# Linear attention and a GLU feed-forward layer on one core: x in a ring with two transfer queues, and some weight sums, loads and stores moved

## The chip, the cores and the metric

The kernel runs on one core of a Trainium2 chip. A core has TensorE (PE, matrix products, with its weight loads listed as PEld), VectorE (DVE), ScalarE (ACT), GpSimd (POOL) and SyncE (SP), each with its own queue of instructions that it takes in order, and 16 DMA engines. DMAs are issued by ACT, POOL or SP. The metric is the time of one execution on the device in microseconds (us); the median of several executions is compared.

## What is computed

q, k and v are float32 of shape (8, 8, 576, 64): batch, head, sequence, head dimension. All weights are float32 as well.

```python
kv = np.einsum('bhsd,bhse->bhde', k, v)
out = np.einsum('bhsd,bhde->bhse', q, kv)
rms = np.sqrt(np.mean(out * out, axis=-1, keepdims=True) + 1e-06)
out = out / rms * g_norm
x = out.transpose(0, 2, 1, 3).reshape(8 * 576, 512)      # 4608 tokens
gate = 1.0 / (1.0 + np.exp(-(x @ w_gate)))               # 512 x 1536
val = x @ w_val                                          # 512 x 1536
y = (gate * val) @ w_out                                 # 1536 x 512
```

## The kernel before

**Chunks and batches.** The feed-forward part runs over 9 chunks (c = 0 to 8) of 512 tokens. A batch of the attention gives 576 tokens, so batches and chunks don't end together. Batches 0 and 1 come at the start; the attention of batch c + 1 is woven into chunk c, for c = 1 to 6. Chunks 7 and 8 have no attention beside them.

**Products.** Chunk 0 is computed with plain matrix products. Chunks 2 to 8 use a fast scheme of the Strassen kind in both layers: the blocks of the matrices are added and subtracted first, and 26 products of these sums take the place of 32. In the first layer (`first_layer_fast`, L926) there are three blocks j of 26 products each, numbered p = 26 j + i; in the second layer (`second_layer_fast`, L1032) there are 26 products with the index i, done in the order 0, 3, 1, 2, 6, 4, 5, 7, 8 and so on up. Chunk 1 has the fast first layer and a plain second one (`second_layer_plain`, L1005). After a product, `combine` adds its PSUM tile to outputs and to temporaries: copies on ACT (L893), sums on DVE (L897) and gate products on POOL (L889, with the sigmoid on ACT, L886). A PSUM tile that later products go on with is first copied or added away; the copy after product 4 of the second layer and the product 7 that goes on in the same tile are such a pair.

**Sums of the inputs.** The sums of x for a chunk (18 operations on DVE, L825 and L827) are made in the second layer of the chunk before. They are put at step p0 of this layer, two a step up to the sum number `two`, then one a step. The sums of the first-layer weights (28 for each block j, `w1_sums`, L739, on POOL) are made once. Those for block 2 are all queued before chunk 1 begins. The weights and their sums are then stored to DRAM in chunk 1 (`keep_w1`, L753, by POOL), and from chunk 2 on they are read back in four granules per block (`load_granule`, L765, by POOL), of 768 or 896 KB. A granule is loaded when the products of the one before it in its place are done. The second-layer weights come the same way (`load_w`, L971).

**Attention.** `feed(c + 1)` gives the steps of a batch, and lists of places hang each on a product. The k and v of a batch come by `load_late`, called at the end of the chunk before: eight main loads (L118), then four smaller ones for the rest of the sequence (L123), all on SP. The q of a pair of heads comes by `load_q` (L104), also on SP, issued when the turn of the pair before is done; so it stands behind these loads in SP's queue. For two pairs of heads at a time, `two_pairs` computes the outputs and their norm, and `x_turn` brings them into the layout that the products want: two transposes on DVE (L432) into `xTs`, then DMAs within SBUF into the tile of x of a chunk (L442, SP). These break at the ends of chunks, so that one `x_turn` has four to six of them. The first two pairs of heads have their `x_turn`s in the first layer, the other two theirs in the second layer, after the 5th and 6th step (`at2` 4 and 5; in chunk 1, 4 and 8).

**Stores.** Each row block of y is stored by SP (L495, L502); only the last one's left half in chunk 8 is shared by SP and ACT.

Of the kernel before, what the change touches and what calls it, by code (L numbers as in the profile page):

```python
# [10 lines left out]
FP32 = mybir.dt.float32  # L11
# [9 lines left out]
def kernel(  # L21
# [11 lines left out]
    nc = tc.nc  # L33
# [75 lines left out]
    def load_late(b):  # L109


        if b >= B:
            return
        mains = {}
        for n in range(NHP):
            for name, src in (("k", k), ("v", v)):
                mains[n, name] = t = kv_place(len(mains))
                nc.sync.dma_start(out=t.rearrange("p (h c) -> p h c", h=2),  # L118
                                  in_=src[b, 2 * n:2 * n + 2, 0:S4].rearrange("h (p j) d -> p h (j d)", j=NK4))
        rest = kv_place(len(mains))  # L120
        for i, src in enumerate((k, v)):
            for r in range(2):
                nc.sync.dma_start(out=rest[PH * r:PH * r + PH, GH * i:GH * i + GH].rearrange("p (h d) -> p h d", d=HD),  # L123
                                  in_=src[b, NHP * r:NHP * r + NHP, S4:S].rearrange("h p d -> p h d"))
        kv_late[b] = mains, rest

# [128 lines left out]
    nc.scalar.activation(out=sb.tile([P, 1], FP32, name="unused", bufs=1), in_=eps, func=AF.Sqrt)  # L255


    xT = {}

    def chunk(c):  # L260
        if c not in xT:
            xT[c] = sb.tile([P, NMT, G], FP32, tag="xT", name="xT", bufs=3)
        return xT[c]

    def attention(n, at_ps):
# [88 lines left out]
    def feed(b):  # L354
# [30 lines left out]
            if e == 1:  # L385
                load_q(n + 1)

        def two_pairs(n0):


            d = {}
            ms = sb.tile([P, NQ, NJ], FP32, tag="ms2", name="ms2", bufs=1)
            sq = sqs[:, 0:2 * S].rearrange("p (r c) -> p r c", r=NQ)
            units = [slice(NJ // 2 * i, NJ // 2 * (i + 1)) for i in range(2)]

            def by_head(t):
                return t.rearrange("p r (n d) -> p r n d", d=HD)

            def u_mm():
                d["u"] = u = at_ps()[:, 0:NQ, 0:2 * QC]  # L400
                for which in range(2):
                    for g in range(JH):
                        for i in range(NC):
                            for r in range(NQ):
                                for e in range(2):
                                    c, o = NJ * HD * e + QC * i + PH * g, HD * (JH * which + g)
                                    nc.tensor.matmul(u[HD * e:HD * e + HD, r, o:o + HD],  # L407
                                                     qTs[QB * r:QB * r + QB, (n0 + which) % 2, c:c + PH],
                                                     kvq[QB * r:QB * r + QB, (n0 + which) % NHP, NC * e + i],
                                                     start=(i == 0), stop=(i == NC - 1))  # L410

            def u_square():
                nc.scalar.activation(out=sq, in_=d["u"], func=AF.Square)

            def u_sum(i):
                nc.vector.tensor_reduce(out=ms[:, :, units[i]], in_=by_head(sq)[:, :, units[i]], axis=AX.X, op=ALU.add)

            def u_root():
                nc.scalar.activation(out=ms, in_=ms, func=AF.Sqrt, bias=eps, scale=1.0 / HD)

            def u_norm(i):
                if i == 0:
                    nc.vector.reciprocal(ms, ms)
                m_ = ms[:, :, units[i]]
                nc.vector.tensor_tensor(out=by_head(sq)[:, :, units[i]], in0=by_head(d["u"])[:, :, units[i]],
                                        in1=m_.unsqueeze(3).to_broadcast([P, NQ, NJ // 2, HD]), op=ALU.mult)

            def x_turn(i):


                for which in range(2):
                    nc.vector.transpose(xTs[:, i, which],  # L432
                                        sq.rearrange("p r (w g i c) -> p w i r g c", w=2, g=JH, i=NC)[:, which, i])
                m = n0 % NHP
                for j in range(2):
                    for e in range(2):
                        p0, p1 = HD * e + QB * j, HD * e + QB * i
                        s0 = 0
                        while s0 < S // 2:
                            c, o = divmod(S * b + S // 2 * j + s0, G)  # L440
                            n_ = min(G - o, S // 2 - s0)
                            nc.sync.dma_start(out=chunk(c)[p1:p1 + QB, m:m + 2, o:o + n_],  # L442
                                              in_=xTs[p0:p0 + QB, i, :, s0:s0 + n_])
                            s0 += n_

            return ([u_mm, u_square, lambda: u_sum(0), lambda: u_sum(1), u_root, lambda: u_norm(0), lambda: u_norm(1)] +
                    [lambda i=i: x_turn(i) for i in range(NC)])
# [4 lines left out]
        n0 = NHP * b  # L452
        kv = [kv_mm] + [lambda i=i: kv_copies(i, range(3)) for i in range(2 * NC)]
        t0, t1, t2, t3 = (turns_of(n0 + i) for i in range(4))
        u0, u1 = two_pairs(n0), two_pairs(n0 + 2)
        first = list(zip((1, 5, 14, 22, 27, 29, 30, 31, 32, 33, 37, 38, 46, 47, 49, 52, 53, 53, 55, 56, 57, 60, 61, 63),
                         t0 + t1 + u0[:1] + t2[:1] + u0[1:2] + t2[1:] + u0[2:5] + t3[:1] + u0[5:6] + t3[1:] + u0[6:] +
                         u1[:7]))
# [269 lines left out]
    NPA = len(PARTS)  # L728
    GW = 7 * 2 * P

    w1_more = [[] for _ in range(N3)]

    def w1_slot(j, s_):
        return w1[:, j, s_].rearrange("p g c -> p (g c)") if s_ < 4 * NMT else w1_more[j][s_ - 4 * NMT]

    def w1_sums(j):
        for v in W_ORDER:
            x, sign, y = SUMS[v]
            nc.gpsimd.tensor_tensor(out=w1_slot(j, w_at[v]), in0=w1_slot(j, w_at[x]), in1=w1_slot(j, w_at[y]),  # L739
                                    op=op_of(sign))  # L740

    def w1_places(part):
        return sorted(w_at[PRODUCTS1[i][1]] for i in PARTS[part])

    def keep_w1(j):
        for part in range(NPA):
            places, k_ = w1_places(part), 0
            while k_ < len(places):
                n, s_ = 1, places[k_]
                while s_ < 4 * NMT and k_ + n < len(places) and places[k_ + n] == s_ + n < 4 * NMT:  # L750
                    n += 1
                src = w1[:, j, s_:s_ + n].rearrange("p s g c -> p (s g c)") if s_ < 4 * NMT else w1_slot(j, s_)
                nc.gpsimd.dma_start(out=kept1[j, part][:, 2 * P * k_:2 * P * (k_ + n)], in_=src)  # L753
                k_ += n

    w1_flat = w1.rearrange("p j s g c -> p (j s g c)")
# [82 lines left out]
    for f in range(0, NFT - 2, 2):  # L839
# [8 lines left out]
        if raw_ctx and not to_convert:  # L848
# [6 lines left out]
            more_sgs = [sums.tile([P, G], FP32, name=f"sg{6 + i}") for i in range(2)]  # L855
            w1_more[2] = [t[:, 2 * P * i:2 * P * i + 2 * P] for t in ring_more + more_sgs
                          for i in range(t.shape[1] // (2 * P))]
            w1_sums(2)
            x_early = deque(x_sums(1))
    assert raw_ctx is None  # L860
    kept3 = kept_pool.tile([18, P, N3 * DH], FP32, name="kept3")
# [45 lines left out]
    def first_layer_fast(c, at):  # L907
        for f in range(NFT):
            gv_tile(c, f)
        for j in range(N3):  # L910
            o = {f"t{n}": pair(temps[:, i]) for i, n in enumerate((0, 1, 8, 9))}
            for n in (3, 1, 2, 0):
# [5 lines left out]
            for i, (name, hv, wv, steps) in enumerate(PRODUCTS1):  # L918
# [15 lines left out]
                        h_fill.popleft()[1]()  # L934
                if c > 1:
                    g_ = NPA * (N3 * (c - 2) + j) + part
                    if i == PARTS[part][-1] and p < NPR * N3 - 1:
                        load_granule(g_ + NPA)
                    k_, r = divmod(p - 20, 2)
                    if r == 0 and 0 <= k_ < NR:  # L940
                        load_w((c - 2) * NS + k_)
                elif p in (NPR, 2 * NPR):
                    keep_w1(j - 1)
                elif p == 2 * NPR + HALF:
                    for g_ in range(NPA):
                        load_granule(g_)
            if c > 1:
                h_fill.extend(h_sums(j, slice(SUMS_FIRST) if j else slice(None)))

# [47 lines left out]

    def second_layer_plain(c, at):
        keep_w1(N3 - 1)
        order_ = [block(l, j) for j in range(N3) for l in (0, 2, 1, 3)]  # L1000
        for t in range(NT):
            i = free.popleft()
            ps = bank(i)
            for n, f in enumerate(order_):
                nc.tensor.matmul(ps, gv[c, f][:, tok[t]], w2[:, f, :], start=(n == 0), stop=(n == NFT - 1),  # L1005
                                 skip_group_check=True)
                for step in at.get(NFT * t + n, ()):
                    step()
            ot = sg_tile()
# [5 lines left out]
    def second_layer_fast(c, at):  # L1015
        o = {f"t{n}": temps[:, i, 0:DH] for i, n in enumerate((0, 1, 8, 9))}
        rows = [sg_tile() for _ in range(NT)]
        for t in range(NT):
            for n in range(2):
                o[f"o{2 * t + n}"] = rows[t][:, DH * n:DH * n + DH]  # L1020
        regions, used, done = {}, {}, count()
        dones = {18: 0, 22: 1, 24: 2, 25: 3}

        def product(i, js):
# [10 lines left out]
        def finish(i):  # L1035
# [6 lines left out]
                load_granule(NPA * N3 * (c - 1) + NPA - 1)  # L1042
            if i in dones:
                t = dones[i]
                if c == NG - 1 and t == NT - 1:
                    store(c, t, rows[t], slice(0, DH), (nc.sync, nc.scalar))
                else:
                    store(c, t, rows[t])
            elif c == NG - 1 and i == 23:
                store(c, NT - 1, rows[NT - 1], slice(DH, DM))  # L1050
            for step in at.get(next(done), ()):
                step()
            sums_of_h(2)
# [47 lines left out]
    for c in range(1, NG):  # L1101
# [5 lines left out]
            for p, step in zip((4, 8) if c == 1 else (4, 5), then):  # L1107
                at2.setdefault(p, []).append(step)
        if c + 1 < NG:
            p0, two = (23, 18) if c == 1 else (12, 8) if c + 1 < B else (6, 0)  # L1110
            p = p0
            for n, step in enumerate(lambda n=n, c=c: x_sum(c + 1, n) for n in range(len(X_SUMS))):
                at2.setdefault(p, []).append(step)
# [38 lines left out]
```

## Time and profile before

| | us |
|---|---|
| median of 6 runs | 1043.68 |
| lowest and highest | 1037.52, 1044.73 |
| the profiled execution | 1044.73 |
| its span, first to last instruction | 1042.6 |
| PE busy | 1019.8 (98%) |
| DVE busy | 720.1 (69%) |
| POOL busy | 606.3 (58%) |
| ACT busy | 348.5 (33%) |
| mean granted clock of PE | 0.995 of full |
| DMA, over the span | 203.31 MB, mean 195 GB/s |

The profiled execution is one of the six, the slowest; 2.1 us of it lie outside of its span. Busy time counts the work of an engine and not its waits, its branches or the DMAs that it issues. In the lines of the profile an arrow `out<-in` names what an instruction writes and reads, an `L` number is a line of the kernel, and a bracket at the end of a timeline line says how long the engine was idle before it and what ended that. "SPq" and "ACTq" are DMAs issued by SP and ACT. Chunk c = 1 begins at 165 us, c = 2 at 282.5, c = 3 at 394, c = 4 at 506, c = 5 at 616, c = 6 at 725, c = 7 at 835.5 and c = 8 at 936.5; the last product ends at 1037.5.

### The profile page before, as it was taken

What the parts mean: (1) busy time and instruction counts of PE and PEld (TensorE: products, weight loads), DVE (VectorE), ACT (ScalarE), POOL (GpSimd) and SP (SyncE); (2) the same over time, 40 slices, a digit from 0 to 9 for tenths busy, and PEclk for the clock granted to TensorE, in tenths of its full rate; (3) what the DMA queues carried; (4) which work ended last, traced back from release to release, by engine and by line L of the source; (5) the groups of instructions that cost most, each with busy time, mean ns of one, the idle gap of its engine ahead of it and who ended that gap; (6) DMA issues with size and microseconds to landing.
All of it is one profiled execution on the core that took longest, in us unless ns stands there. A gap on an engine that the chain in (4) does not pass through costs nothing.

```text
span 1042.6 us, 18190 instructions
## 1 busy us (share of the span) xinstructions
PE 1019.8 (98%) x6854; PEld 818.3 (78%) x6854; DVE 720.1 (69%) x1188; ACT 348.5 (33%) x604; POOL 606.3 (58%) x991
## 2 busy tenths in 40 slices
PE   8999999999999999999999999999999999999998
PEld 7644447785588878888888888888888888888886
DVE  3799899585767854786567666875578655765672
ACT  3554422341144402541154214520444033203320
POOL 0000999977229660887078524964296629753973
PEclk9999999999999999999999999999999999999999
DMA  9966311358878566865777558745774646454624
GB/s 250 264 221 207 121 41 53 119 184 310 286 258 282 154 184 199 283 207 162 215 240 237 153 167 271 247 157 164 239 272 154 192 160 247 146 167 157 237 75 117
DMA packets 98406, 203.31 MB, mean 195 GB/s; under 512 B 29840, under 2 KB 69008, under 8 KB 98320
## 3 DMA queue, kind: packets, MB, share of 16 engines
q0 software_dynamic: 28048, 138.43, 39.2%
q1 hardware_dynamic: 70016, 63.66, 21.2%
q8 instruction: 54, 0.88, 0.4%
q14 instruction: 32, 0.26, 0.1%
q10 hardware_dynamic: 256, 0.07, 0.0%
HBM read 168.30 MB, written 26.74 MB: 187 GB/s over the span
## 4 chain that ended last, share of the span: by engine, by line
PE 55%; DMA 4%; DVE 4%; SPq 1%; issue 1%; DVEq 0%
PE mm L926 38%; PE mm L1032 15%; DMA xT<-xTs 3%; DMA q<-in_q_dram 2%; DVE xs L825 2%; PE at L407 1%; SPq L442 1%; DVE sg L897 1%; DVE xs L827 1%; DVE temps L897 0%; PE at L366 0%; DVE h L897 0%; DVE h_more L721 0%; PE at L372 0%; DVE xTs L432 0%
## 5 line engine op out<-in xcount | busy, mean ns | idle before, releaser
L926 PE MATMUL mm<-xs,w 128*128 128x256 f32 x1428 | 334.1, 380 | 3.1 <-DVE h L897 3.1
L926 PEld LDWEIGHTS mm<-xs,w 128*128 128x128 f32 x1428 | 270.5, 190 | 42.9 <-DVE h L897 4.3
L926 PE MATMUL mm<-xT,w 128*128 128x256 f32 x948 | 230.9, 381 | 0.0
L926 PEld LDWEIGHTS mm<-xT,w 128*128 128x128 f32 x948 | 179.3, 190 | 25.8 <-issue 1.3
L897 DVE TENSOR_TENSOR sg<-sg,mm 128x512 f32<-128x512 f32 (+1 forms) x169 | 98.6, 607 | 105.5 <-PE mm L926 46.7
L765 POOL DMA_DIRECT2D w<-kept x84 | 46.8, 558 | 206.2 <-PE mm L926 205.9
L1032 PE MATMUL mm<-w,h 128*128 128x256 f32 x558 | 127.7, 380 | 3.9 <-DVE sg L897 3.3
L893 ACT COPY temps<-mm 128x512 f32<-128x512 f32 (+1 forms) x124 | 65.0, 549 | 176.8 <-PE mm L926 93.6
L1032 PEld LDWEIGHTS mm<-w,h 128*128 128x128 f32 x558 | 105.6, 190 | 20.0 <-DVE sg L897 4.9
L889 POOL TENSOR_TENSOR h<-h,sg 128x512 f32<-128x512 f32 x72 | 92.6, 1305 | 31.1 <-ACT sg L886 23.6
L721 POOL TENSOR_TENSOR h<-h 128x128 f32<-128x128 f32 x189 | 97.7, 529 | 14.5 <-DVE h_more L721 11.4
L886 ACT ACTIVATE sg<-sg 128x512 f32<-128x512 f32 x96 | 59.9, 632 | 112.0 <-DVE sg L897 111.6
L1032 PE MATMUL mm<-w,h_more 128*128 128x256 f32 x390 | 88.9, 379 | 0.0
L893 ACT COPY sg<-mm 128x512 f32<-128x512 f32 (+1 forms) x107 | 54.8, 522 | 84.3 <-PE mm L1032 42.7
L1032 PEld LDWEIGHTS mm<-w,h_more 128*128 128x128 f32 x390 | 74.1, 190 | 10.1
L560 PE MATMUL mm<-xT,w 128*128 128x512 f32 x176 | 77.7, 594 | 0.0
L897 DVE TENSOR_TENSOR temps<-temps,mm 128x512 f32<-128x512 f32 (+1 forms) x93 | 58.1, 625 | 24.0 <-PE mm L1032 16.0
L739 POOL TENSOR_TENSOR h_more<-w 128x256 f32<-128x256 f32 x10 | 12.9, 1302 | 100.6 <-PE at L366 100.6
L893 ACT COPY h<-mm 128x512 f32<-128x512 f32 x48 | 28.1, 586 | 125.4 <-PE mm L926 124.0
L897 DVE TENSOR_TENSOR temps<-mm,temps 128x512 f32<-128x512 f32 (+1 forms) x62 | 38.8, 626 | 44.2 <-PE mm L1032 22.1
L721 POOL TENSOR_TENSOR h_more<-h 128x128 f32<-128x128 f32 x105 | 51.6, 494 | 29.8 <-DVE h L889 26.3
L971 POOL DMA_DIRECT2D w<-kept x102 | 63.0, 618 | 2.2 <-issue 1.9
(144 smaller groups left out, 1397.2 us busy)
## 6 DMA issues: line engine op xcount, KB each, us to landing
w<-kept POOLq DMA_DIRECT2D x102, 384.0 KB, 5.0
w<-kept POOLq DMA_DIRECT2D x42, 896.0 KB, 5.5
w<-kept POOLq DMA_DIRECT2D x42, 768.0 KB, 5.1
w_ring<-kept POOLq DMA_DIRECT2D x24, 384.0 KB, 4.9
out_dram<-sg SPq DMA_DIRECT2D x110, 64.0 KB, 1.7
q<-in_q_dram SPq DMA_DIRECT2D x24, 288.0 KB, 4.3
st<-in_moe_w_gate_dram SPq DMA_DIRECT2D x12, 512.0 KB, 5.5
st<-in_moe_w_val_dram SPq DMA_DIRECT2D x12, 512.0 KB, 6.3
```

What stands on the lines that cost most here:

```text
L560: nc.tensor.matmul(self.ps[i], w[("wg", "wv")[i], self.f][:, m, :], xT[self.c][:, m, :], start=(m == 0), stop=(m == NMT - 1), skip_group_c ...
L721: ops.append((eng, lambda v=v, x=x, sign=sign, y=y, eng=eng: eng.tensor_tensor(out=h_form(v, j), in0=h_form(x, j), in1=h_form(y, j), op=op ...
L739: nc.gpsimd.tensor_tensor(out=w1_slot(j, w_at[v]), in0=w1_slot(j, w_at[x]), in1=w1_slot(j, w_at[y]), op=op_of(sign))
L765: nc.gpsimd.dma_start(out=granule(g)[:, 0:n], in_=kept1[g // NPA % N3, g % NPA][:, 0:n])
L825: tt(out=place[v], in0=place[x], in1=place[y], op=op_of(sy))
L886: nc.scalar.activation(out=o["o" + step[1]], in_=o["o" + step[1]], func=AF.Sigmoid)
L889: mult.tensor_tensor(out=o[x], in0=o[x], in1=o[y], op=ALU.mult)
L893: nc.scalar.copy(out=o[out_], in_=o[expr])
L897: tt(out=o[out_], in0=o[x], in1=o[y], op=ALU.add if sign == "+" else ALU.subtract)
L926: nc.tensor.matmul(regions[name][1][:, g], ws[:, g], xf[c][wv], start=(new and g == 0), stop=True, skip_group_check=True)
L971: nc.gpsimd.dma_start(out=ring(i), in_=kept3[i % NS].rearrange("p (j n) -> p j n", j=N3))
L1032: nc.tensor.matmul(regions[name][1], h_form(hv, j), ws[:, j], start=(used[i] and j == 0), stop=(j == N3 - 1), skip_group_check=True)
```

## The change

- The four rest loads of `load_late` (L123) are issued by ACT.
- x is one tile of 3 × 512 tokens, used as a ring. An `x_turn`'s DMAs break only where the ring ends; there are four per `x_turn`, and more for two of the batches. For the second two pairs of heads, those of the second half of the sequence (j = 1) are issued by ACT.
- Of the 28 sums of block 2's weights, 20 are queued at the old place; the other eight come one after each product of block 1 in chunk 1, from p = 26 on.
- The stores of `keep_w1` go to SP, one a product, from a list. The four granule loads at p = 2·26 + HALF are two there and two in the second layer.
- From chunk 2 on, for block 0 while attention is woven in, the granule loads behind parts 0 and 1 wait three products longer.
- The x sums in chunks 2 to 6 begin at step 14 instead of 12, and go singly from the twelfth on instead of the eighth.
- In the last chunk, all stores are shared by SP and ACT.

```diff
@@ load_late
-                nc.sync.dma_start(out=rest[PH * r:PH * r + PH, GH * i:GH * i + GH].rearrange("p (h d) -> p h d", d=HD),
+                nc.scalar.dma_start(out=rest[PH * r:PH * r + PH, GH * i:GH * i + GH].rearrange("p (h d) -> p h d", d=HD),
                                   in_=src[b, NHP * r:NHP * r + NHP, S4:S].rearrange("h p d -> p h d"))
...
-    xT = {}
+    NX = 3
+    xT_ring = const.tile([P, NMT, NX * G], FP32, name="xT")
+    xT = {c: xT_ring[:, :, G * (c % NX):G * (c % NX + 1)] for c in range(NG)}
...
@@ two_pairs
-                            c, o = divmod(S * b + S // 2 * j + s0, G)
-                            n_ = min(G - o, S // 2 - s0)
-                            nc.sync.dma_start(out=chunk(c)[p1:p1 + QB, m:m + 2, o:o + n_],
-                                              in_=xTs[p0:p0 + QB, i, :, s0:s0 + n_])
+                            o = (S * b + S // 2 * j + s0) % (NX * G)
+                            n_ = min(NX * G - o, S // 2 - s0)
+                            (nc.sync, queue)[j].dma_start(out=xT_ring[p1:p1 + QB, m:m + 2, o:o + n_],
+                                                          in_=xTs[p0:p0 + QB, i, :, s0:s0 + n_])
...
-        u0, u1 = two_pairs(n0), two_pairs(n0 + 2)
+        u0, u1 = two_pairs(n0), two_pairs(n0 + 2, nc.scalar)
...
@@ the weights' sums and stores
+    W1_FIRST = 20
-    def w1_sums(j):
-        for v in W_ORDER:
+    def w1_sums(j, some=slice(None)):
+        for v in W_ORDER[some]:
...
+    keeping = deque()
...
-                nc.gpsimd.dma_start(out=kept1[j, part][:, 2 * P * k_:2 * P * (k_ + n)], in_=src)
+                keeping.append(lambda out=kept1[j, part][:, 2 * P * k_:2 * P * (k_ + n)], src=src:
+                               nc.sync.dma_start(out=out, in_=src))
...
-            w1_sums(2)
+            w1_sums(2, slice(W1_FIRST))
...
@@ first_layer_fast
-                    if i == PARTS[part][-1] and p < NPR * N3 - 1:
-                        load_granule(g_ + NPA)
+                    if p < NPR * N3 - 1:
+                        wait = (3 if part < 2 else 0) if j == 0 and c + 1 < B else 0
+                        if wait and i == PARTS[part][-1]:
+                            held[i + wait] = g_ + NPA
+                        elif i == PARTS[part][-1]:
+                            load_granule(g_ + NPA)
+                        if j == 0 and i in held:
+                            load_granule(held.pop(i))
...
-                elif p in (NPR, 2 * NPR):
-                    keep_w1(j - 1)
-                elif p == 2 * NPR + HALF:
-                    for g_ in range(NPA):
-                        load_granule(g_)
+                else:
+                    if p in (NPR, 2 * NPR):
+                        keep_w1(j - 1)
+                    if keeping:
+                        keeping.popleft()()
+                    if NPR <= p < NPR + len(W_ORDER) - W1_FIRST:
+                        w1_sums(2, slice(W1_FIRST + p - NPR, W1_FIRST + p - NPR + 1))
+                    if p == 2 * NPR + HALF:
+                        load_granule(0)
+                        load_granule(1)
...
@@ second_layer_plain
+        while keeping:
+            keeping.popleft()()
+        loads = {4: 2, 8: 3}
...
+                if NFT * t + n in loads:
+                    load_granule(loads[NFT * t + n])
...
@@ second_layer_fast
+        ends = (nc.sync, nc.scalar) if c == NG - 1 else (nc.sync,)
...
-                if c == NG - 1 and t == NT - 1:
-                    store(c, t, rows[t], slice(0, DH), (nc.sync, nc.scalar))
-                else:
-                    store(c, t, rows[t])
+                store(c, t, rows[t], slice(0, DH if c == NG - 1 and t == NT - 1 else DM), ends)
             elif c == NG - 1 and i == 23:
-                store(c, NT - 1, rows[NT - 1], slice(DH, DM))
+                store(c, NT - 1, rows[NT - 1], slice(DH, DM), ends)
...
@@ the loop over chunks
-            p0, two = (23, 18) if c == 1 else (12, 8) if c + 1 < B else (6, 0)
+            p0, two = (23, 18) if c == 1 else (14, 12) if c + 1 < B else (6, 0)
```

More of the change, by code (lines that the diff above doesn't have):

```diff
@@ L255 @@
     nc.scalar.activation(out=sb.tile([P, 1], FP32, name="unused", bufs=1), in_=eps, func=AF.Sqrt)
-    xT = {}
+    NX = 3
+    xT_ring = const.tile([P, NMT, NX * G], FP32, name="xT")
+    xT = {c: xT_ring[:, :, G * (c % NX):G * (c % NX + 1)] for c in range(NG)}
     def chunk(c):
-        if c not in xT:
-            xT[c] = sb.tile([P, NMT, G], FP32, tag="xT", name="xT", bufs=3)
         return xT[c]
@@ L386, in turn, with two_pairs @@
                 load_q(n + 1)
-        def two_pairs(n0):
+        def two_pairs(n0, queue=nc.sync):
             d = {}
@@ L909, in first_layer_fast @@
             gv_tile(c, f)
+        held = {}
         for j in range(N3):
```

## The prediction, made before the changed kernel had run

> **What bounds the kernel now.** I read the busy shares first, then the chain of waits, then the waits by group, then windows, and at last the timeline around every gap of TensorE (PE).
>
> ```profile
> PE 1019.8 (98%) x6854; PEld 818.3 (78%) x6854; DVE 720.1 (69%) x1188; ACT 348.5 (33%) x604; POOL 606.3 (58%) x991
> ...
> PE 55%; DMA 4%; DVE 4%; SPq 1%; issue 1%; DVEq 0%
> ```
>
> PE is the bound: 22.8 us of the 1042.6 us span are not PE work. The change adds and removes no matmul, so it can only gain what PE loses, some 2%. The second line is the chain of waits: what is not PE is DMA and VectorE (DVE), so the losses are data that comes late. The windows view by chunk shows where they are (columns: window, its length, then busy time and instructions of PE, PEld, DVE, ACT, POOL, granted clock, DMA share, GB/s):
>
> ```profile
> 199.00:203.50 4.50, 4.50 (x14) 3.42 (x13) 2.89 (x5) 0.83 (x3) 4.50 (x10) 0.62 0.72 270
> ...
> 394.00:506.00 112.00, 109.24 (x840) 94.59 (x839) 76.64 (x139) 37.84 (x68) 65.03 (x115) 1.00 0.65 207
> ...
> 835.00:936.00 101.00, 101.00 (x470) 88.91 (x469) 64.99 (x114) 25.82 (x48) 66.84 (x115) 1.00 0.56 183
> ```
>
> Chunk 7 (835 to 936), which has no attention beside it, loses nothing. Chunk 3 (394 to 506) loses 2.76 us; chunks 2 to 6 are like it. At 199 us the clock fell. The groups of waits name the reasons:
>
> ```profile
> DVE qTs L383 <- DMA q<-in_q_dram: 20.0, 5, 5.5
> ...
> DVE xs L825 <- DMA xT<-xTs: 13.8, 5, 7.3
> ...
> PE mm L1032 <- DVE sg L897: 4.6, 5, 1.4
> ...
> PE mm L926 <- ACT sg L893: 2.6, 1, 2.6
> ```
>
> And the timeline, on the three kinds of stall and on the ScalarE (ACT) copy that matters below:
>
> ```profile
> 198.62 1.13 PE L926 MATMUL mm<-xs,h_more 128*128 128x256 f32 x4 [2.58 <-ACT sg L893]
> ...
> 413.76 0.45 PE L372 MATMUL at<-h_more 64*64 64x64 f32 x12 [1.44 <-DMA h_more<-in_v_dram]
> ...
> 496.68 3.50 PE L1032 MATMUL mm<-w,h 128*128 128x256 f32 x15 [1.00 <-DVE sg L897]
> ```
> ```profile
> 193.01 4.93 POOL L889 TENSOR_TENSOR h<-h,sg 128x512 f32<-128x512 f32 x4
> ...
> 478.88 0.37 ACT L893 COPY temps<-mm 128x256 f32<-128x256 f32 x1 [0.92 <-PE mm L1032]
> 479.43 0.57 POOL L971 DMA_DIRECT2D w_ring<-kept  x1
> 479.47 2.50 SPq L442 DMA_DIRECT2D xT<-xTs  x4
> ```
>
> **What the Trainium skill says.** "DMA: Bandwidth & Descriptors", Issuing engines are not separate DMA queues: transfers started by several engines run on the same 16 DMA engines, and only issue time is saved. That is what is short here: the twelve x transfers of chunk 3 leave SyncE (SP) one after another, 0.64 us apart, from 479.47 to 487.2, and need 4 to 6 us each to land. "Perfetto Trace Analysis", DMA Instruction — HWDGE (DVE, Sync): the sequencer is held until the descriptors are made, and the generator is locked meanwhile. The trace agrees for ACT: two DMAs, issued at 0.75 and 1.34 (0.56 and 0.61 us), and its next instruction at 1.98. It doesn't show SP and ACT hindering one another: at the tail both issue from 1037.99 and keep their 0.46 (SP) and 0.35 to 0.43 us (ACT). "TensorE: Matmul & The Clock Gate", What's actually happening: the clock is halved after an idle window of some 3.4 us, which runs freely. Here a gap of 2.58 us was followed by 3.4 us at half speed (199.97 to 203.39), while gaps of 1.0 to 1.7 us were followed by none.
>
> **Part by part.** Losses are measured as PE's start-to-start time above its usual 0.216 us per matmul, so they hold the restart too.
>
> Chunk 1's sums. GpSimd (POOL) does the 28 sums for block 2 (L739, 0.83 us apart) from 169.87 to 193.05, and only then the four gate products of block 0 (L889, 193.01 to 197.94). The ACT copy behind them in its queue starts at 197.98, and PE waits for that copy: 2.74 us, and then half clock costs 2.1 us more: 4.84. Eight sums less ahead make 8 × 0.83 = 6.6 us; the copy is then free at some 191.4 and waits for its own product alone, which it did from about 194.7 on; it ends by 195.3, before the 196.04 at which PE wants it. Gain 4.84. The eight sums follow one by one beside block 1; POOL's kept stores (L753, 0.7 us each) go to SP, whose queue there has nothing urgent (24 + 23 + 22 stores at some 0.62 us). Nothing else is late: block 2 starts 67 us on. Taken at nothing.
>
> The rest loads of k and v (L123), which stand ahead of q's loads on SP. The four take 3.4 to 4.2 us of SP (in chunk 5, 732.85 to 736.95) and q is issued at 737.05, landed 745.06; PE then lost 1.99 us at 746. With these on ACT, q is issued about 3.5 us sooner. Stalls that this removes: chunk 2 1.28, chunk 3 1.76 + 0.58, chunk 6 1.99: 5.6 us. The granule loads held back by three products (2.6 us) leave q the DMA engines as well. On ACT the four come after the copy of product 16, where ACT is idle for some 10 us: free. Only from chunk 1 to 2 they stand ahead of a copy: 283.2 + 4 × 0.65 to 0.8 + 0.59 makes 286.4 to 287.0 against 286.0: loss 0.4 to 1.0, taken as 0.9.
>
> x in a ring: the transfers no longer break at the ends of chunks, 8 per layer instead of 12 (two batches cross the ring's end and have more). Of these, SP keeps four (the first halves) and ACT takes four. The x sums (L825, L827), which stood in DVE's queue from step 12, begin at step 14. For chunk 3 before: step-12 sums wait for the ninth transfer, issued 484.62, landed 490.41; DVE is then behind, the difference L897 ends at 496.6, and product 19 waits. After: SP's four are issued by 482.0 and landed by 486 to 488, the sums start at about 492, and the difference is done at some 495.7, wanted 496.8. The x-sum stalls were 0.88 + 1.62 (chunk 2), 1.27, 1.01, 1.61, 0.42: 6.8 us, all gained.
>
> But ACT now has the DMAs in its queue. In the second layer its order becomes: copy of product 6, two x DMAs, copy of product 4, two x DMAs, next copy (the order of the changed program). The DMAs wait for DVE's transposes (L432), which end at 479.46 in chunk 3; two issues of 0.64 make 480.74; the copy of product 4 (478.88 before) ends at 481.15 with its 0.37. Product 7 goes on in the PSUM tile that this copy reads, and PE wants to start it at 480.0: 1.19 us late. By the same sum chunk 2 loses 1.01, 4 0.99, 5 and 6 1.0; with 0.1 each for the restart, 5.7 us. These gaps are too short to halve the clock, by what the trace shows. This is a new wait, and I take it in full. The trace of before has no x DMA on ACT: below, ACT issues at 0.35 to 0.43 as at the tail (stall 0.7 each, loss 3.7); above, see the rivals.
>
> Last stores: SP's row-3 stores are issued to 1040.5 behind row 2's, the last lands at 1041.66; ACT's land at 1040.14. With both queues for all four rows about 1.5 us less.
>
> Sum: 4.84 + 5.6 + 6.8 + 1.5 = 18.7 gained, 5.7 + 0.9 = 6.6 lost: 12.1 us. Span 1042.6 − 12.1 = 1030.5, and with 2.1 around it 1032.6 for such an execution. The profiled execution (1044.73) is the slowest of six; against their median, 1043.68 − 12.1 = 1031.5.
>
> **Rivals.**
> 1. The new ACT wait doesn't cost: issues at the tail's 0.4 us, or transposes that come earlier, because DVE has less to wait for. For it: 0.35 us rows of ACT at the tail. Against: x rows on SP are 0.59 to 0.61 throughout, of the same shape. Net 17 to 18: 1026.
> 2. ACT and SP share the generator while both send x, so an ACT issue lasts 1.2: two more per layer cost 1.2 more, 5 × 1.2 = 6. Net 6: 1037.5. For it: the lock in the skill. Against: the tail.
> 3. Slower. The same wait, with ACT issues of 1.4 us or more (SP rows in chunk 1 took 1.0 to 1.7). Then product 7 is 2.7 us late or more in each of five layers, and gaps of that length halve the clock, as at 199.97: 2.7 + 0.1 + 2.1 = 4.9 each, 24.5 in all, and with 0.9 more than the 18.7 gained: some 7 slower, 1050. It decides from about 1.4 us per issue: below, the clock stays and gains win.
> 4. The change does less than it says: q lands no sooner, since its transfers wait for the DMA engines (share 0.65, 8 us from issue to landing) and not for the issue; 5.6 fall to 1 or 2, and part of the x sums' gain with them. Net 5 to 7: 1038.
>
> **How the numbers follow.** Forecast 0.50; rival 1 0.17, 2 0.12, 3 0.07, 4 0.14. The main case reaches from 1028 to 1035 (ACT loss 3.7 to 8, one or two stalls left). Leaving out rival 3 and the outer parts of 1 and 4, the range is 1025 to 1040. About 0.5% (5.2 us) can be told from no change: faster is below 1038.5, which holds the forecast, rival 1 and over half of 2 and 4: 0.83; same 0.10; slower 0.07.
>
> **What would show it.** Right: no gap near 195 to 200 and a clock of 1.00 there; no PE wait on q or v at the starts of chunks 2, 3, 6; no PE wait at L1032 on DVE's sg; a new PE wait at L1032, about 1.2 us, in five second layers, some 9 us after each one's start, released by ACT's copy (L893) that stands behind L442 rows on ACT; last stores ending about 2.5 us after the last product. Wrong: ACT rows of L442 well off 0.6 us, a half clock in second layers, or q stalls that stay.

## The result, and the profile after

| | before | after |
|---|---|---|
| median, us | 1041.78 (71 runs) | 1032.48 (34 runs) |
| lowest to highest | 1033.61 to 1050.58 | 1030.96 to 1041.91 |
| profiled execution, its span | 1044.73, 1042.6 | 1032.53, 1030.7 |

The ratio is 0.9922, 95% interval 0.9909 to 0.9934. The page of the changed kernel, its busy shares and the last chain of waits:

```profile
PE 1016.7 (99%) x6854; PEld 816.2 (79%) x6854; DVE 718.1 (70%) x1188; ACT 348.0 (34%) x604; POOL 567.5 (55%) x922
...
PE 22%; DVE 0%; ACTq 0%; issue 0%; ACT 0%; DVEq 0%
```

PE has its 6854 matmuls as before, and 14.0 us of the span are left that are not PE. The chain can be followed back over the last 22% of the span only, to 793 us, and in this stretch an ACT copy behind x DMAs (chunk 6) stands in it. The windows by chunk say where the time went (columns as before: window, length, busy PE, PEld, DVE, ACT, POOL, clock, DMA share, GB/s):

```profile
165.00:276.00 111.00, 111.00 (x691) 79.46 (x690) 80.92 (x131) 31.66 (x50) 48.26 (x62) 1.00 0.62 213
...
386.00:495.50 109.50, 108.20 (x838) 94.09 (x838) 75.86 (x140) 37.86 (x69) 65.02 (x115) 1.00 0.67 212
...
824.00:925.00 101.00, 101.00 (x469) 88.61 (x468) 64.93 (x114) 25.81 (x48) 66.87 (x115) 1.00 0.56 182
```

Chunk 1 (165 to 276) has no gap and a full clock. Chunk 3 (386 to 495.5) still loses 1.3 us; chunks 2, 5 and 6 lose 1.1 to 1.3, and chunk 4 loses 2.5, of which 1.3 is a gap in its attention that the last section comes back to. The groups of waits say to what, and also how far q has come forward:

```profile
DVE qTs L383 <- DMA q<-in_q_dram: 11.1, 5, 2.7
...
PE mm L1054 <- ACT temps L897: 5.7, 5, 1.3
```

The waits of L1032 (now L1054) on DVE's sg and those for q and v are gone; five waits on ACT's copy have come. The timeline of chunk 3's second layer shows the first of the order that makes them:

```profile
466.89 1.54 DVE L432 STREAM_TRANSPOSE xTs<-sqs 128x288 f32<-128x288 f32 x4
...
467.74 2.58 SPq L442 DMA_DIRECT2D xT<-xTs  x4
467.75 1.50 ACTq L442 DMA_DIRECT2D xT<-xTs  x2
...
469.28 0.37 ACT L897 COPY temps<-mm 128x256 f32<-128x256 f32 x1 [3.05 <-DVE sg L901]
469.37 1.25 ACTq L442 DMA_DIRECT2D xT<-xTs  x2
...
469.71 2.64 PE L1054 MATMUL mm<-w,h_more 128*128 128x256 f32 x11 [1.29 <-ACT temps L897]
```

DVE's transposes end the wait of the DMAs, two DMAs take ACT 1.50 us, only then comes the copy, and PE starts product 7 when the copy is done, 1.29 us idle. The bracket of the copy names a sum on DVE, but that sum had ended at 468.94; the copy starts at 469.28, 0.04 us after the second DMA's issue has ended.

Both programs have the same matmuls in the same order, so the start of the same matmul can be compared between the two traces. The lead of the changed kernel, worked out at the layers' ends, and by how much each stretch changed it:

| stretch | lead at its end, us | change |
|---|---|---|
| chunk 0 and the first attention | 2.56 | +2.56 |
| chunk 1, first layer | 7.27 | +4.71 |
| chunk 1, second layer | 7.27 | 0 |
| first layers of chunks 2 to 6 | | +0.94, +2.36, −0.07, −0.43, +1.79: +4.59 |
| second layers of chunks 2 to 6 | | +1.16, −0.29, −0.35, +0.24, −0.94: −0.18 |
| chunks 7 and 8 | 11.43 | −0.24 |
| from the last product to the end | 11.9 | +0.47 |

The first row is no effect of the change. In the profiled execution of before, PE waited 1.94 us for v at 17.97 and ran at a clock of 0.81 in the window 15.5 to 24.5:

```profile
17.97 0.92 PE L276 MATMUL two<-v,k 96*64 96x64 f32 x24 [1.94 <-DMA v<-in_v_dram]
```
```profile
15.50:24.50 9.00, 7.06 (x104) 6.64 (x104) 5.61 (x8) 2.91 (x4) 0.00 (x0) 0.81 0.87 232
```

A second profile of before, shown below under before_again, has a clock of 1.00 there and is 3.0 us ahead of the first by 22.5. Without this row the lead is 9.3 us, which is also the difference of the medians. The row of second layers is the one to remember: 6.8 us of waits for x went, and ACT's copies took all of it back.

### The profile page after: what moved, and what is told of

Read it like the earlier page. It is cut to its first block, busy times and chain, and to the rows that moved or that the text cites. A ratio compares the mean times of both kernels' runs of the same rounds, so it can differ in the third digit from the quotient of the medians.

```text
span 1030.7 us, 18177 instructions
## 1 busy us (share of the span) xinstructions
PE 1016.7 (99%) x6854; PEld 816.2 (79%) x6854; DVE 718.1 (70%) x1188; ACT 348.0 (34%) x604; POOL 567.5 (55%) x922
## 5 line engine op out<-in xcount | busy, mean ns | idle before, releaser
L901 DVE TENSOR_TENSOR sg<-sg,mm 128x512 f32<-128x512 f32 (+1 forms) x169 | 98.5, 607 | 110.6 <-PE mm L931 54.0
L1054 PE MATMUL mm<-w,h 128*128 128x256 f32 x558 | 126.6, 379 | 0.0
L1054 PEld LDWEIGHTS mm<-w,h 128*128 128x128 f32 x558 | 106.0, 190 | 14.4
L721 POOL TENSOR_TENSOR h<-h 128x128 f32<-128x128 f32 x189 | 95.4, 518 | 14.5 <-DVE h_more L721 11.4
L1054 PE MATMUL mm<-w,h_more 128*128 128x256 f32 x390 | 90.1, 380 | 5.7 <-ACT temps L897 5.7
L1054 PEld LDWEIGHTS mm<-w,h_more 128*128 128x128 f32 x390 | 73.7, 190 | 17.5 <-ACT temps L897 7.7
L901 DVE TENSOR_TENSOR temps<-temps,mm 128x512 f32<-128x512 f32 (+1 forms) x93 | 58.2, 626 | 24.2 <-PE mm L1054 15.6
L901 DVE TENSOR_TENSOR temps<-mm,temps 128x512 f32<-128x512 f32 (+1 forms) x62 | 38.9, 627 | 50.6 <-PE mm L1054 22.5
```

The costliest lines, as they stand in the source:

```text
L721: ops.append((eng, lambda v=v, x=x, sign=sign, y=y, eng=eng: eng.tensor_tensor(out=h_form(v, j), in0=h_form(x, j), in1=h_form(y, j), op=op ...
L901: tt(out=o[out_], in0=o[x], in1=o[y], op=ALU.add if sign == "+" else ALU.subtract)
L1054: nc.tensor.matmul(regions[name][1], h_form(hv, j), ws[:, j], start=(used[i] and j == 0), stop=(j == N3 - 1), skip_group_check=True)
```

## The experiments

For each run the time that PE lost in gaps, by kind, from its one profile. A loss is taken from start to start above the usual 0.216 us per matmul, from 0.1 us on, and without the slower matmuls behind it; so it is up to 0.2 us more than the idle time in the brackets of the timelines:

| | span | chunk 1 | q, v at chunk starts | L1032 on DVE | on ACT's copy | ratio to before, interval |
|---|---|---|---|---|---|---|
| before | 1042.6 | 2.74 | 5.2 | 6.2 | 0 | 1 |
| before_again | 1041.4 | 2.48 | 7.7 | 5.1 | 0 | one run |
| before_place | 1038.4 | 2.72 | 7.5 | 0.7 | 0 | 0.9936 (0.9899 to 0.9972) |
| before_act | 1044.8 | 2.42 | 6.2 | 0.3 | 7.7 | 1.0039 (1.0018 to 1.0060) |
| after | 1030.7 | 0 | 0 | 0 | 6.5 | 0.9922 (0.9909 to 0.9934) |
| sums_28 | 1034.1 | 2.51 | 0 | 0 | 6.5 | 0.9965 (0.9949 to 0.9981) |
| rest_sync | 1034.4 | 0 | 4.1 | 0 | 6.5 | 0.9970 (0.9953 to 0.9987) |
| no_hold | 1033.3 | 0 | 1.6 | 0 | 6.5 | 0.9932 (0.9907 to 0.9956) |
| tail_sync | 1031.4 | 0 | 0 | 0 | 6.5 | one run |
| x_on_sync | 1028.3 | 0 | 1.0 | 0 | 0 | 0.9894 (0.9865 to 0.9923) |
| act_later | 1027.4 | 0 | 2.5 | 0 | 0 | 0.9874 (0.9844 to 0.9905) |
| sync_12 | 1037.2 | 0 | 4.1 | 2.7 | 0 | 0.9942 (0.9920 to 0.9964) |
| act_later_12 | 1026.7 | 0 | 1.5 | 1.7 | 0 | 0.9879 (0.9847 to 0.9911) |
| hold_6 | 1027.0 | 0 | 1.5 | 0 | 0 | 0.9878 (0.9846 to 0.9910) |

**The new wait: all transfers on SyncE.**

```diff
-        u0, u1 = two_pairs(n0), two_pairs(n0 + 2, nc.scalar)
+        u0, u1 = two_pairs(n0), two_pairs(n0 + 2)
```

> The changed kernel with all x transfers on SyncE again, everything else as changed. Theory: ScalarE's x DMAs ahead of the copy of product 4 cost 1.25 to 1.46 us of TensorE in each of five second layers (6.5 us with the profile of the changed kernel), and the x sums at step 14 need no second queue: SyncE's eight leave within 5.1 us from 467.7 and land by about 478, the sums begin at 481. So the five gaps at L1054 go, none takes their place, and the span is about 1024.2 against 1030.7. Rival: the second queue is what freed the x sums; then the waits of L1054 on VectorE's sg come back, 4 to 7 us, and the span stays near 1030.

The five gaps went and none came back at L1054; the sums of x at step 14 don't need the second queue. In chunk 3 PE now runs through product 7 without a pause:

```profile
465.57 5.78 PE L1054 MATMUL mm<-w,h_more 128*128 128x256 f32 x26
```

Compared start by start with the changed kernel's trace, each of the five second layers is 1.36 to 1.56 us shorter, 7.0 in all. The span is 1028.3 and not 1024.2, for in this execution PE lost 2.6 us to a gap in chunk 4's attention that no semaphore explains, with half clock behind it, and 1.0 us for q in chunk 3. Gaps of both kinds stand in other kernels' profiles too. But all five runs of this kernel have spans above 1024.2 (1026.0 to 1029.2), and the interval of its ratio overlaps the changed kernel's; so whether transfers on SyncE alone cost something elsewhere stays open.

**The new wait: the order in ACT's queue.** The DMAs of the first `x_turn` for ACT are put into a list and issued with those of the second, which stand behind the copy of product 4.

```diff
-                            (nc.sync, queue)[j].dma_start(out=xT_ring[p1:p1 + QB, m:m + 2, o:o + n_],
-                                                          in_=xTs[p0:p0 + QB, i, :, s0:s0 + n_])
+                            def send(out=xT_ring[p1:p1 + QB, m:m + 2, o:o + n_], in_=xTs[p0:p0 + QB, i, :, s0:s0 + n_],
+                                     q_=(nc.sync, queue)[j]):
+                                q_.dma_start(out=out, in_=in_)
+                            if queue is not nc.sync and j and i == 0:
+                                later.append(send)
+                            else:
+                                while j and later:
+                                    later.pop(0)()
+                                send()
```

> The changed kernel with two queues kept, but ScalarE's two DMAs of the first x_turn issued with those of the second, behind the copy of product 4. Theory (order in ScalarE's queue is the price): the five gaps go, span about 1024.2, as with all transfers on SyncE. Rival (x DMAs on ScalarE cost wherever they stand, by holding the generator or the next copy): gaps of about 1 us remain at the next copy, span 1027 to 1031.

ACT's part of chunk 3's timeline:

```profile
468.30 0.37 ACT L905 COPY temps<-mm 128x256 f32<-128x256 f32 x1
469.60 0.37 ACT L905 COPY temps<-mm 128x256 f32<-128x256 f32 x1 [0.92 <-PE mm L1062]
470.19 2.87 ACTq L445 DMA_DIRECT2D xT<-xTs  x4
...
474.78 0.37 ACT L905 COPY temps<-mm 128x256 f32<-128x256 f32 x1 [4.81 <-PE mm L1062]
```

The copy now waits for its own product (0.92 us idle, released by PE), the four DMAs take ACT 2.87 us behind it, and the next copy has 1.7 us to spare before it. No gap at the next copy: the rival falls. The second layers are shorter by the same 1.36 to 1.56 us, 7.0 in all. The ratio of 0.9874 has an interval that just lies below the changed kernel's: with the same work on the same two queues, the place in the queue is the price. The span was expected at 1024.2 and is 1027.4, because the last main load of v came 2.3 us late in chunk 3 and half clock followed.

**Two queues alone, on the kernel before.**

```diff
-            nc.sync.dma_start(out=chunk(c)[p1:p1 + QB, m:m + 2, o:o + n_],
+            (nc.sync, queue)[j].dma_start(out=chunk(c)[p1:p1 + QB, m:m + 2, o:o + n_],
...
-        u0, u1 = two_pairs(n0), two_pairs(n0 + 2)
+        u0, u1 = two_pairs(n0), two_pairs(n0 + 2, nc.scalar)
```

> The kernel before, with the x transfers of the second half of the sequence of the second two pairs (j = 1) on ScalarE and nothing else: no ring, old places. Theory: the wait is traded. The gaps on VectorE's sg (6.8 us in the profile of before) go for the most part, and in their place come waits on ScalarE's copy, four of 1.25 us and one of about 2.5 in chunk 2, whose batch has four such transfers per x_turn: 7.9 us with restarts; against before -1 to +3 us, ratio 1.00. Rival (two queues are a gain by themselves): 0.994 or below.

It is slower than before by 0.4%, 4 us (interval 2 to 6), somewhat more than the theory gave. Chunk 2, where four DMAs stand ahead of the copy:

```profile
366.30 2.80 ACTq L442 DMA_DIRECT2D xT<-xTs  x4
...
369.14 0.37 ACT L893 COPY temps<-mm 128x256 f32<-128x256 f32 x1 [4.14 <-issue]
...
369.57 1.59 PEld L1032 LDWEIGHTS mm<-w,h_more 128*128 128x128 f32 x8 [2.78 <-ACT temps L893]
369.57 1.78 PE L1032 MATMUL mm<-w,h_more 128*128 128x256 f32 x7 [2.38 <-ACT temps L893]
```

Four issues of 0.70 us on average make PE idle for 2.38 us; in the layers with two it is idle for 1.08 to 1.30. The gap grows with the number of DMAs in the queue ahead of the copy, as the mechanism says. Of the waits on DVE's sg 0.3 us is left, so the trade is shown: some 6 us of one kind for 7.7 of the other.

**The place of the x sums alone, on the kernel before.**

```diff
-            p0, two = (23, 18) if c == 1 else (12, 8) if c + 1 < B else (6, 0)
+            p0, two = (23, 18) if c == 1 else (14, 12) if c + 1 < B else (6, 0)
```

> The kernel before with the x sums of chunks 2 to 6 from step 14, singly from the twelfth on, and nothing else: no ring, twelve x transfers on SyncE. Theory (the place alone frees the sums): the last transfers that the sums need land near 491 to 492 in chunk 3's time, the sums come to VectorE 2.6 us later than before, at about 492; the waits of L1032 on VectorE's sg (6.8 us in the profile of before) go, ratio near 0.994. Rival (the twelve transfers are still late): at least half of these waits stay, 3 us or more, ratio 0.997 or above.

One gap of 0.65 us, in chunk 2, is left of 6.2. No ring and no second queue were needed for the rest. The ratio of 0.9936 agrees: this one line is worth about 6.7 us (interval 3 to 10.5).

**The ring's fewer transfers, with the old place.** On top of x_on_sync:

```diff
-            p0, two = (23, 18) if c == 1 else (14, 12) if c + 1 < B else (6, 0)
+            p0, two = (23, 18) if c == 1 else (12, 8) if c + 1 < B else (6, 0)
```

> All x transfers on SyncE as in x_on_sync, and the x sums again from step 12, singly from the eighth on, as before the change. What is left of the change for x is the ring with its eight transfers in place of twelve. Theory (the number of transfers was the cause): the last that the sums need are issued 2.6 us sooner than before the change and land about when VectorE comes to the sums; at most one or two gaps of 0.5 us at L1054, span 1024 to 1026. Rival (the place of the sums was the cause): waits of L1054 on VectorE's sg in most of the five layers, 3 to 7 us in all, span 1028 to 1031.

Five gaps at L1054, 0.99, 0.40, 0.62, 0.45 and 0.28: in each layer, less than the rival said, more than the theory. The span of 1037.2 also holds late q and v and two stretches at half clock. Why the gaps stay shows DVE's timeline in chunk 3. There SP's sixth transfer, the last of the first halves, was issued at 472.89 and landed at 478.34:

```profile
478.92 0.68 DVE L901 TENSOR_TENSOR sg<-temps 128x256 f32<-128x256 f32 x1
479.53 1.26 DVE L829 TENSOR_TENSOR xs<-xT 128x256 f32<-128x256 f32 x2
480.83 0.56 DVE L829 TENSOR_TENSOR xs<-xT,xs 128x256 f32<-128x256 f32 x1
481.31 0.67 DVE L831 SCALAR_TENSOR_TENSOR xs<-xT,xs 128x256 f32<-128x256 f32 x1
...
484.36 0.41 DVE L901 TENSOR_TENSOR sg<-mm,sg 128x256 f32<-128x256 f32 x1
484.70 1.00 DVE L901 TENSOR_TENSOR sg<-sg,temps 128x256 f32<-128x256 f32 x2
485.63 0.41 DVE L901 TENSOR_TENSOR sg<-temps,mm 128x256 f32<-128x256 f32 x1
```
```profile
484.82 1.03 PE L1054 MATMUL mm<-w,h 128*128 128x256 f32 x4
486.09 2.21 PE L1054 MATMUL mm<-w,h 128*128 128x256 f32 x9 [0.24 <-DVE sg L901]
```

The first x sum starts at 479.53, over a microsecond after its data landed. From there to the last L901 line DVE has no idle time: eight x sums stand in its queue ahead of the difference that product 19 wants, and that difference ends at 486.04. It is DVE's queue and not a transfer that is late.

**The same question with two queues.** act_later with the line of the diff just shown.

> act_later (two queues, ScalarE's x DMAs behind the copy) with the x sums again from step 12, singly from the eighth on. In sync_12 the data of chunk 3's sums had landed (478.3) when VectorE came to them (479.5), and product 19 was still 0.4 us late. Theory (the sums' place is the cause: eight of them stand in VectorE's queue ahead of the difference that product 19 wants): the gaps at L1054 stay as in sync_12, 0.3 to 1.0 us in each of the five layers, 2.5 to 3.5 us in all, though the transfers land 2 us sooner. Rival (landing is the cause): they go, below 0.5 us in all.

0.13, 0.41, 0.45, 0.45 and 0.28 us, 1.7 in all (2.2 with the restarts): below the 2.5 to 3.5 that were expected, and well above the rival's 0.5. In chunks 3, 5 and 6 the gaps are those of sync_12 to 0.01 us; in chunk 2 and partly in 4 the earlier landing helps (0.99 to 0.13, 0.62 to 0.45). So the waits for x had two causes: the late landing and DVE's own queue. Earlier landing takes 6.2 us to 2.7 with the ring on one queue and to 1.7 with the second queue (from one profile each; the second profile of before starts from 5.1). The rest is DVE's queue, and there only the place helped. The place alone also covers most of the landing. In the time the two places can't be told apart here (0.9874 and 0.9879).

**Chunk 1's sums.**

```diff
-    W1_FIRST = 20
+    W1_FIRST = 28
```

> The changed kernel with all 28 sums of block 2's weights queued before chunk 1 again; the stores stay on SyncE. Theory: the gate products of block 0 are behind the sums on GpSimd and end near 198; TensorE waits some 2.7 us for ScalarE's copy and then runs at half clock to the end of the window: 4.8 us more than the changed kernel, ratio near 0.997. Rival (the stores on GpSimd were part of it): half of that or less, no half clock.

The gap came back, 2.34 us of idle PE, and the half clock with it. The windows view of the stretch (clock 0.69), and PE's first line there:

```profile
194.00:199.50 5.50, 4.43 (x13) 3.57 (x14) 3.39 (x5) 1.56 (x3) 0.40 (x1) 0.69 0.67 229
```
```profile
195.07 1.56 PE L931 MATMUL mm<-xs,h_more 128*128 128x256 f32 x4 [2.34 <-ACT sg L897]
```

The ratio rose by 0.0043, 4.5 us. The eight sums are the cause; with the stores on SP and the sums at the old place the gap is as long as in the four kernels that don't move them (2.51 us against 2.42 to 2.74).

**The rest loads.**

```diff
-                nc.scalar.dma_start(out=rest[PH * r:PH * r + PH, GH * i:GH * i + GH].rearrange("p (h d) -> p h d", d=HD),
+                nc.sync.dma_start(out=rest[PH * r:PH * r + PH, GH * i:GH * i + GH].rearrange("p (h d) -> p h d", d=HD),
```

> The changed kernel with the four rest loads of k and v on SyncE again, behind the main loads and ahead of q. Theory (the rest loads delay q, by SyncE's issue time and by 256 KB more in the crowded stretch at a chunk's start; on ScalarE they left some 15 us before it): waits of TensorE on q or v come back at the starts of chunks 2, 3 and 6 or others like them, 3 to 6 us in all, span about 1035, ratio near 0.996. Rival (the granule loads held back did it, the queue of the rest loads doesn't matter): no such waits, ratio 0.992 as with the whole change.

SP's timeline at the start of chunk 3, and what PE says:

```profile
390.93 1.42 SPq L123 DMA_DIRECT2D h_more<-in_k_dram  x2
392.40 2.59 SPq L123 DMA_DIRECT2D h_more<-in_v_dram  x2
395.09 0.54 SPq L104 DMA_DIRECT2D q<-in_q_dram  x1
```
```profile
404.85 2.01 PE L931 MATMUL mm<-xs,w 128*128 128x256 f32 x4 [2.12 <-DVE h L901]
```

q was issued 4.2 us behind the first rest load, landed at 403.62, and DVE's transpose of q (L383) held up the sum on DVE that PE waited for. The ratio rose by 0.0048, 5.0 us, and the two intervals lie apart. The one profile alone would not show it: sync_12, which has the rest loads on ACT, lost 4.1 us at its chunk starts as well. In the changed kernel the same four loads leave ACT at 372 to 376, when chunk 2's second layer is still running, some 12 us before the main loads; so they are also out of the crowded stretch, not only out of SP's queue. These two effects weren't taken apart.

**The granule loads held back.**

```diff
-                        wait = (3 if part < 2 else 0) if j == 0 and c + 1 < B else 0
+                        wait = 0
```

> The changed kernel with the granule loads of block 0 not held back. Theory (q and v are late through the rest loads alone): below 1 us of new waits at the chunk starts, ratio 0.992 to 0.993. Rival (the DMA engines are full at a chunk's start, and 0.9 and 0.8 MB of granules ahead of the last main loads and q delay them): waits of 1 to 3 us at the starts of two or more chunks, 2 to 6 us in all, ratio 0.994 to 0.998.

One gap of 1.57 us (chunk 6) came, and the ratio moved by 0.0010, within its interval. The theory's bound was 1 us, the rival's 2; what the delay is worth stays open.

Six products in place of three, on top of act_later:

```diff
-                        wait = (3 if part < 2 else 0) if j == 0 and c + 1 < B else 0
+                        wait = (6 if part < 2 else 0) if j == 0 and c + 1 < B else 0
```

> The kernel with ScalarE's DMAs behind the copy (act_later), and the granule loads of block 0 held back by six products instead of three. In act_later the last main load of v for chunk 3's attention landed 12.8 us after its issue, 2.5 us late. Theory (the DMA engines are full there, and a granule isn't wanted for another 17 products): the wait at the start of chunk 3 goes or halves, nothing is late behind it, span 1023 to 1025. Rival (the granules come too late for block 1 then): new waits at L931 early in block 1, span 1027 or more.

Inconclusive: chunk 3 lost 1.48 us for q in place of 2.5 for v, the ratio is the same as act_later's, and no new wait for granules came.

**A second profile of before, and the last stores.** The first of these two is the kernel before without any edit.

> The kernel before once more, for a second profile. Theory: the waits set by order (chunk 1's gate products, 4.6 to 4.9 us; the x sums, 6 to 7 us) come again within 0.5 us each, the waits for q and v at the chunk starts come again in sum (4 to 8 us), but at other chunks and sizes. Rival: the x sums' waits vary as well, by 2 us or more.

The waits for x came to 5.1 us against 6.2 and shifted between layers by up to 0.9, the chunk-1 gap was 2.48 against 2.74, and the waits for q and v 7.7 against 5.2. So the waits for x vary as well, by 1.1 us, more than the theory's 0.5 and less than the rival's 2. That fits waits which depend on when transfers land; what made this profile differ isn't shown.

```diff
-        ends = (nc.sync, nc.scalar) if c == NG - 1 else (nc.sync,)
+        ends = (nc.sync,)
```

with the two `store` calls of before.

> The changed kernel with the last chunk's stores as before (SyncE alone but for half of the last row block). Theory, from the two traces: VectorE's last sum to the end of the span is 5.06 us before and 4.59 after; so 0.4 to 0.6 us longer than in the changed kernel, not the 1.5 that the last stores' landing suggests.

From DVE's last sum (1026.15) to the end of the span (1031.4) it took 5.25 us, against 4.59 in the changed kernel: 0.66 us, somewhat over the upper end.

## Why the prediction was right, and where its sum was not

The time, 1031.5, was 1.0 us off, and in part by luck: the gain of 12.1 us was too large by 2.8, and the median of six that it was taken from lay 1.9 us above that of 71, so two errors nearly cancel. The span, forecast as 1030.5 and measured as 1030.7, is luck too: of the 11.9 us between the profiled spans, 2.56 were lost at the start of that one execution of before. The mechanisms hold for the most part. Two terms were mis-sized, ACT's copy and the last stores, and the reason given for the x sums was half of it.

| step of the prediction | predicted, us | measured by the lead |
|---|---|---|
| chunk 1's sums | +4.84 | +4.71 |
| q and the rest loads, with the loss from chunk 1 to 2 | +5.6 − 0.9 = +4.7 | +4.59 |
| x sums against ACT's new wait | +6.8 − 5.7 = +1.1 | −0.18 |
| last stores | +1.5 | +0.47 |
| chunks 7 and 8 | 0 | −0.24 |
| sum | 12.1 | 9.35 |

- Chunk 1: shown. Putting the sums back brought gap and half clock back.
- The rest loads: shown by the times of rest_sync, with 5.0 us. The near agreement in the table hides two misses: the gain was 5.0 and not 5.6, the loss from chunk 1 to 2 0.43 and not 0.9. That these waits go for good is too much: kernels with the change have 0 to 2.5 us of them from profile to profile (4.1 in sync_12).
- ACT's copy: the mechanism is shown, from both sides (x_on_sync and act_later remove it, before_act makes it). Its size was short by 1.3 us: 7.0 with the restarts, for 5.7. Two issues took 1.50 us in chunk 3 for the 1.28 taken from SP's rows, and the hand-overs between DMA, copy and matmul, some 0.05 us each, were left out.
- Rival 1 (no such cost) fell. Rivals 2 and 3 asked for issues of 1.2 and of 1.4 us; ACT's, while SP issued beside it, took 0.65 and 0.81, then 0.59 and 0.62. Rival 4 fell for q in the profile of the changed kernel.
- The x sums: right in size, but the reason was only half of it. The prediction let them come late through the ninth transfer; the runs show the transfers and DVE's own queue, and that the new place alone does nearly all (6.2 to 0.7 us). It priced the ring and the second queue together with the place and couldn't see that the queue, which carries the whole cost, wasn't needed.
- The last stores: the landing came 1.1 us earlier for the 1.5 predicted (3.0 us after DVE's last sum for 4.1), but from the last landing to the end of the span it took 1.6 us in place of 0.9. The term was taken from the landing alone.
- Three readings are a little off, without weight in the sum. The four rest loads took SP 2.8 to 4.4 us in chunks 2 to 6, not 3.4 to 4.2; those from 732.85 on belong to chunk 6; and five stalls of 0.7 us with 0.1 each for the restart make 4.0 and not 3.7.

The version that beats both keeps the change and issues ACT's x DMAs behind the copy (act_later: 1026.71 us median, 0.9874).

## What to carry to other kernels

A DMA given to a compute engine stands in that engine's queue with its wait for data and its issue, and everything behind it stands there too; look for the next copy that the tensor engine wants, and put the DMA behind it. When a wait for data goes, ask which of several edits does it, and try the one that costs nothing first: here two steps later in a list did what the second queue was meant for. And look at a second profile before a chance wait is priced: here one held 2.56 us at its start that the next one didn't, and the waits for q and v were 5.2 us in one and 7.7 in the other.

## What was not expected of the hardware

The clock was halved after shorter gaps than the prediction allowed. In no_hold, PE was idle for 1.25 us:

```profile
548.30 0.32 PE L407 MATMUL at<-kvq,qTs 32*64 32x64 f32 x2 [1.25 <-issue]
548.55 1.80 PE L931 MATMUL mm<-xT,w 128*128 128x256 f32 x4
```

and the windows view right behind it shows a clock of 0.53:

```profile
549.00:552.50 3.50, 3.50 (x11) 2.72 (x9) 1.41 (x2) 1.91 (x3) 3.40 (x8) 0.53 0.43 79
```

In the changed kernel PE was idle for 1.30 us at the same place and the clock stayed at 1.00. The gaps that ACT's copy made and that cost 1.24 to 1.47 us were followed by no halving in 29 cases (five layers of five profiles, four of before_act), nor were two longer ones in before_act, of 2.38 us in chunk 2 and of 2.61 us for v in chunk 3. So the length of a gap alone doesn't decide. By the clock records of the traces, each halved stretch before the last product lasted 3.4 us, or twice that in sync_12 and x_on_sync. "TensorE: Matmul & The Clock Gate" of the Trainium skill, section What's actually happening, has an idle window of some 3.4 us that runs freely. The length of the stretches fits it, the gaps don't: no gap here but one (4.09 us in sync_12) was as long, and the measured halvings decide.

All profiles have a gap in chunk 4 within the attention's small matmuls (L407) that is listed as "issue", up to 4.1 us long. In all 14 profiles (20 gaps), a 16 KB packet of the instruction queue, of about 1 us, had begun 2.2 to 2.9 us before the gap ended. There are 54 such packets in an execution, though, and only one or two have such a gap behind them. That PE waits for its instructions there is likely, and not shown: no run changed it.
